# Weight sums moved from GpSimd to VectorE in single steps, four sets in the first pair, output weights loaded at two earlier places

## The chip, the cores and the metric

The kernel runs on one core of one Trainium2 chip. The metric is the device time of one execution in microseconds (us), lower is better. Five engines work side by side, each through its own list in order: TensorE (PE), VectorE (DVE), ScalarE (ACT), GpSimd (POOL) and SyncE (SP), which here issues nearly all transfers between the chip's memory and the on-chip buffers.

## The reference

Attention in chunks of 64 keys, then a feed-forward block with RMS norm and SiLU gate, in float32. N = 4608 tokens, model width 512, inner width 1536.

```python
scores = scale * np.matmul(q_c, k_c.transpose(0, 1, 2, 4, 3))   # chunks of 64
attn = softmax(scores)
x = np.matmul(attn, v_c)        # heads side by side: 4608 x 512
xn = x / sqrt(mean(x * x) + 1e-6) * rms_g
g, val = xn @ w_gate, xn @ w_val
out = (g * sigmoid(g) * val) @ w_out
```

## The kernel before

**Tiles and pairs.** Tokens go in nine tiles of 512. Tile 0 is done plainly while the weights are brought into a split form (a high part that the PE takes exactly and a rest, three matmuls for one product). The other eight form four pairs, b = 0 to 3. A pair multiplies as a 2x2 block matrix with seven products, P1 to P7, instead of eight; each needs its own sums of weight blocks and of inputs.

**The first pair, b = 0,** still takes its gate and value weights plainly: two blocks (tiles) of twelve inner columns f, `gate_into`, ps_g and ps_v in the profile (L587). Its output stage, `down_pair`, uses seven products with the output weights wo (L1066), which `out_load` (L972) brings from their split home osd, 1 MB each. **From b = 1 on** `up_pair` (L854) takes seven products over pieces i = 0 to 5, with weights wr that `ring_load` (L846) brings from the split home wsd three ahead, 1 MB for two products, then `down_pair`.

**The weight sets.** For P3, P5, P6 and P7 of each piece i, `sides(i)` loads the weight blocks (w<-wfd, L751, two transfers of 512 KB), forms four sums on POOL (L745), and `save_split` then does four times: a cast on ACT (L774), a store of the high part (wsd<-side, L775), a subtraction on DVE (L776), a store of the rest (wsd<-w, L777). The high part, `side`, lies in a pool of four buffers that it shares with `gh`, the high part of the output stage's inputs.

**Attention of the next tiles** runs in between, by units of 256 tokens: scores (PE ps_s, L266), maxima, subtraction and sums on DVE (L336, L337, L348), exponential on ACT (L343), a transpose on DVE (e, L360), which goes through memory (away_e<-e, L362, then eight transfers eT<-away_e, L371), then values (PE ps_o, L388). The result xu goes through the norm and through memory too (away_x, x<-away_x, L423, L430).

**Order.** A step counter runs one step per group of matmuls: 48 steps for a pair's first stage. Tables (SIDE_AT, LATE_SIDE_AT, UNIT_AT, PAIR_AT and others) say at which step a part of the side work is written down. PE's order is that of the code; a scheduler orders the other engines in the first stages, all are in written order in the output stages. Every DMA also waits for the one that stands eight places before it on SP, since eight completion counters go round, and whatever stands behind it on SP waits with it. Steps of SIDE_AT count from the first pair's start; its second block begins at step 24.

Of the kernel before, what the change touches and what calls it, by code (L numbers as in the profile page):

```python
# [43 lines left out]
X_AT = 5, 12, 13, 14, 15, 16, 25, 27, 30  # L44
OUT_AT = -2, 0, 3, 7, 11, 15
SAVE_AT = 5, 9, 13, 17, 21, 25
SIDE_AT = 29, 35, 41
LATE_SIDE_AT = 0, 6, 12
IN_ORDER = {
    mybir.EngineType.PE,  # L50
    mybir.EngineType.Activation,
# [29 lines left out]
def tile_chunk_attn_swiglu(  # L81
# [10 lines left out]
    nc = tc.nc  # L92
# [32 lines left out]
    def urgent():  # L125

        return tc.high_priority(offset=URGENT)
# [600 lines left out]
    def save_up(i):  # L728
        one, two = parts_of(2 * i), parts_of(2 * i + 1)
        save_side(i, P1, one[:, :, :, :KH])  # L730
        save_side(i, P2, one[:, :, :, KH:])
        save_side(i, P4, two[:, :, :, KH:])
# [7 lines left out]
    def sides(i):  # L740

        at = {}

        def total(out, one, two, op):
            nc.gpsimd.tensor_tensor(out, one, two, op=op)  # L745

        def load():
            both = big([P, 2, 2, DM], F32, "w")
            for f in range(2):
                w = both[:, f]  # L750
                nc.sync.dma_start(w.rearrange("p m c -> p (m c)"), wfd[2 * i + f])  # L751
                for half in range(2):
                    at[f + 1, half + 1] = w[:, :, half * KH : (half + 1) * KH]

        def sums():
            total(at[2, 2], at[2, 1], at[2, 2], ALU.add)
            total(at[2, 1], at[1, 1], at[2, 1], ALU.subtract)
            total(at[1, 1], at[2, 2], at[1, 1], ALU.subtract)
            total(at[1, 2], at[1, 2], at[1, 1], ALU.subtract)

        def split():
            save_split(i, P7, at[2, 1])
            save_split(i, P5, at[2, 2])
            save_split(i, P6, at[1, 1])
            save_split(i, P3, at[1, 2])

        return [load, sums, split]

    def save_split(i, p, w):

        n = 7 * i + p
        dst = wsd[n // 2][:, n % 2].rearrange("p (a m c) -> p a m c", a=2, m=2)
        part = tmp.tile([P, 2, KH], F32R, tag="tmp", name="side")
        nc.scalar.copy(part, w)  # L774
        nc.sync.dma_start(dst[:, 0], part.bitcast(F32))  # L775
        nc.vector.tensor_tensor(w.bitcast(F32R), w, part.bitcast(F32), op=ALU.subtract)  # L776
        nc.sync.dma_start(dst[:, 1], w)  # L777

    def big(shape, dtype, name):
        return wts.tile(shape, dtype, tag="wts", name=name)  # L780
# [188 lines left out]
    def out_load(n):  # L969
        t = big([P, PER, 2, OH], F32R, "wo")  # L970
        part = t[:, : osd[n].shape[1]].rearrange("p n a c -> p n (a c)")
        nc.sync.dma_start(part.bitcast(F32), osd[n])  # L972
        return t
# [212 lines left out]
    at = {}  # L1186

    def plan(n, todo):
        at.setdefault(n, []).append(todo)

    for n, u in enumerate(range(4, 10)):
        after_it = LAST_STEPS if u == 9 else PAIR_STEPS
# [3 lines left out]
    for i in range(NPR):  # L1196
# [9 lines left out]
            plan(OUT_AT[i] + (min(k, 2) if OUT_AT[i] >= 0 else 0), part)  # L1206
        plan(SAVE_AT[i], lambda i=i: save_up(i))
    for i, n in enumerate(SIDE_AT):
        for after_it, f in zip((0, 1, 3), sides(i)):
            plan(n + after_it, f)  # L1210

    def before(n):
# [42 lines left out]
    for b in range(NB):  # L1255
        t = 1 + 2 * b
        gts, wos, tt, sums, ready = [], [], [], [], []

        def first_splits():
            for g, _ in gts[:2]:  # L1260
                split_high(g[:, 0, 0], ready)
            split_low(gts[0][0][:, 0, 0], ready[0])

        if b == 0:

            one, two, late = x_sides(x, x2, st)
            for n, f in enumerate(one[:2]):
                plan(UNIT_AT[3] + PAIR_STEPS[-1] + 4 + n, f)
            for n, f in zip(X_AT, one[2:] + two[:1] + two[4:] + two[1:4]):
                plan(2 * UP + n, f)  # L1270
            early = {n: list(todo) for n, todo in enumerate(late)}
            for i, n in enumerate(LATE_SIDE_AT):
                for after_it, f in zip((0, 1, 3), sides(len(SIDE_AT) + i)):
                    early.setdefault(n + after_it, []).append(f)
            step = Steps(at)
            gs = []
            for f in range(NF):
                if f % 2 == 0:
                    gs.append(big([P, 2, 2, TT], F32, "g"))
                gate_into(f, gs[-1][:, f % 2, 0], step, f == NF - 1)  # L1280
            with urgent():
                for dt in range(NDT):
                    x_split(dt, blocks(x)[:, :, dt], slice(0, TT))
            for f in range(NF):
                i = f // 2
                if f % 2 == 0 and sums:
                    sums.pop()()
                end = f == NF - 1
                if end:
                    gts.append((gs[i], None))  # L1290
                    wos.append(out_load(0))
                    wos.append(out_load(1))
                gate_into(f, gs[i][:, f % 2, 1], step, f == 0, first_splits if end else None)
                if f % 2:
                    if end:
                        gts.pop()
                    gts.append((gs[i], sum_later(i, gs[i], tt, sums)))
        else:
            at = early
            early = {}  # L1300
            if b + 1 < NB:
                u = 2 * t + 4
                for n in range(4):
                    home = (lambda: x2) if n > 1 else (lambda: x)
                    for k, f in enumerate(unit_steps(u + n, home)):
                        after_it = LAST_STEPS if b == 1 and n == 3 else PAIR_STEPS
                        at.setdefault(max(PAIR_AT[n] + after_it[k], 0), []).append(f)
                one, two, late = x_sides(x, x2, st)
                for n, f in enumerate(one[:2]):
                    at.setdefault(PAIR_AT[1] + PAIR_STEPS[-1] + 4 + n, []).append(f)  # L1310
                for n, f in zip(X_AT, one[2:] + two[:1] + two[4:] + two[1:4]):
                    at.setdefault(7 * NPR + n, []).append(f)
                early = {n: list(todo) for n, todo in enumerate(late)}
            step = Steps(at)
            for i in range(NPR):
                last_part = first_splits if i == NPR - 1 else None
                gts.append(up_pair(i, step, wos, tt, sums, last_part))
        loaded[0] = 0
        ordered.__exit__(None, None, None)
        ordered = tc.manual_schedule(engines=IN_ORDER)  # L1320
        ordered.__enter__()
        down_pair(t, gts, wos, step, b + 1 < NB, sums, ready)
        ordered.__exit__(None, None, None)
        ordered = tc.manual_schedule(engines={mybir.EngineType.PE})
        ordered.__enter__()
# [53 lines left out]
```

## Time and profile before

| what | value |
|---|---|
| median of 3 runs | 932.96 us (932.84 to 936.49) |
| profiled execution | 933.43 us, span 931.6 us |
| PE busy | 881.9 us of the span |
| DVE busy | 648.1 us |
| ACT busy | 486.5 us |
| POOL busy | 196.1 us, of it 33.5 us in the 24 sums of L745 |
| second block of the first pair | ends at 290.3 us |
| first output stage | to 363 us, then the second pair's first stage |

All other numbers come from the one profiled execution; its own time lies 0.5 us above the median. A row of a timeline has the start in us from the span's start, the length, the engine, the line, the operation, output and inputs without buffer numbers, the size and the count of like instructions run together; in brackets the idle time of the engine ahead of it and what ended it. SPq is SP's own queue: the row is the time over which transfers were issued, not when they landed.

### The profile page before, as it was taken

The page shows a single profiled execution, that of the slowest core. Times are in us where ns is not written, and L with a number is a line of the kernel's source. Part 1 is how long each engine was busy: PE and PEld are TensorE (multiplying, and loading weights), DVE is VectorE, ACT ScalarE, POOL GpSimd, SP SyncE. Part 2 cuts the span into 40 slices and gives each one's busy share as a digit, 9 for nine tenths or more (in the row PEclk, how much of TensorE's full clock was granted, in tenths as well). Part 3 has the DMA queues.
Part 4 walks back from the last instruction along what each step waited for, and adds up shares of the span by engine and source line. Part 5 has one row for each costly group of instructions (what it writes and reads, how often), then busy time and mean ns, then how long its engine had stood idle before and what let it go on. Part 6 is the DMA issues. An engine that isn't in the chain of part 4 may idle for free.

```text
span 931.6 us, 17562 instructions
## 1 busy us (share of the span) xinstructions
PE 881.9 (95%) x6792; PEld 718.4 (77%) x6792; DVE 648.1 (70%) x1030; ACT 486.5 (52%) x807; POOL 196.1 (21%) x165
## 2 busy tenths in 40 slices
PE   4899999999996999895999999999999999999998
PEld 3688888788875787774888887887887878888886
DVE  6999897665863897764565997666668964334776
ACT  5998955445552754442474754444747532222452
POOL 0004020000520003534134001332340013432201
PEclk9799999999998999987999999999999999999999
DMA  9698999876778668897898678676875686335442
GB/s 353 267 349 336 321 334 304 265 242 205 241 251 284 263 242 320 276 312 233 307 332 317 228 279 327 253 215 246 295 241 225 243 336 251 142 138 202 203 159 90
DMA packets 87379, 242.85 MB, mean 261 GB/s; under 512 B 9088, under 2 KB 45440, under 8 KB 71808
## 3 DMA queue, kind: packets, MB, share of 16 engines
q1 hardware_dynamic: 86240, 241.21, 73.0%
q8 instruction: 53, 0.87, 0.4%
q10 hardware_dynamic: 1056, 0.52, 0.2%
q14 instruction: 30, 0.25, 0.1%
HBM read 178.26 MB, written 63.44 MB: 259 GB/s over the span
## 4 chain that ended last, share of the span: by engine, by line
PE 85%; DMA 7%; DVE 3%; ACT 2%; issue 1%; SPq 1%; POOL 0%; DVEq 0%; ACTq 0%; POOLq 0%
PE ps_c L854 11%; PE ps_a L854 10%; PE ps_b L854 10%; PE ps_v L587 8%; PE ps_g L587 8%; PE ps_c L1066 7%; PE ps_a L1066 7%; PE ps_b L1066 6%; PE ps_d L854 6%; PE acc L658 4%; DMA wr<-wsd 3%; PE ps_d L1066 3%; PE ps_o L388 2%; PE ps_s L266 2%; DMA osd<-side 2%
## 5 line engine op out<-in xcount | busy, mean ns | idle before, releaser
L854 PE MATMUL ps_c<-xp,wr 128*128 128x512 f32 x432 | 106.4, 396 | 0.2 <-DMA wr<-wsd 0.2
L854 PE MATMUL ps_a<-xp,wr 128*128 128x512 f32 x432 | 104.8, 390 | 0.6 <-DMA wr<-wsd 0.6
L854 PE MATMUL ps_b<-xp,wr 128*128 128x512 f32 x432 | 104.5, 391 | 0.0
L854 PEld LDWEIGHTS ps_c<-xp,wr 128*128 128x128 f32 x432 | 82.0, 191 | 17.9 <-issue 0.5
L854 PEld LDWEIGHTS ps_a<-xp,wr 128*128 128x128 f32 x432 | 80.9, 188 | 18.5 <-DMA wr<-wsd 1.7
L854 PEld LDWEIGHTS ps_b<-xp,wr 128*128 128x128 f32 x432 | 80.6, 188 | 17.2 <-DVE p L947 0.2
L587 PE MATMUL ps_g<-xh,parts 128*128 128x512 f32 x272 | 91.2, 396 | 0.6 <-ACT xh L512 0.6
L587 PE MATMUL ps_v<-xh,parts 128*128 128x512 f32 x272 | 90.4, 393 | 0.0
L977 ACT CAST gh<-g 128x512 fp32r<-128x512 f32 x96 | 58.2, 621 | 55.8 <-PE ps_b L1066 17.7
L982 DVE TENSOR_TENSOR gl<-g,gh 128x512 fp32r<-128x512 f32 x96 | 65.7, 694 | 26.1 <-PE ps_a L1066 14.4
L854 PE MATMUL ps_d<-xp,wr 128*128 128x512 f32 x216 | 54.9, 405 | 11.2 <-DMA wr<-wsd 11.2
L1066 PE MATMUL ps_a<-gh,wo 128*128 128x512 f32 x192 | 53.9, 396 | 8.1 <-DMA wo<-osd 8.1
L982 DVE TENSOR_TENSOR gl<-tt,gh 128x512 fp32r<-128x512 f32 x72 | 55.8, 787 | 8.0 <-PE ps_a L1066 4.1
L587 PEld LDWEIGHTS ps_g<-xh,parts 128*128 128x128 f32 x272 | 51.7, 190 | 12.0 <-ACT xh L512 1.0
L587 PEld LDWEIGHTS ps_v<-xh,parts 128*128 128x128 f32 x272 | 51.3, 189 | 11.0
L913 ACT ACTIVATE p<-p 128x512 f32<-128x512 f32 x36 | 22.7, 632 | 67.7 <-POOL p L935 50.1
L854 PEld LDWEIGHTS ps_d<-xp,wr 128*128 128x128 f32 x216 | 41.9, 195 | 20.6 <-issue 11.6
L977 ACT CAST gh<-tt 128x512 fp32r<-128x512 f32 x72 | 42.7, 621 | 26.0 <-PE ps_b L1066 12.5
L945 POOL TENSOR_TENSOR g<-u,u 128x512 f32<-128x512 f32 x18 | 23.2, 1287 | 155.2 <-DVE u L941 71.1
L935 POOL TENSOR_TENSOR p<-p,p 128x512 f32<-128x512 f32 x36 | 46.9, 1314 | 36.5 <-DVE p L934 29.5
L587 PE MATMUL ps_g<-xl,parts 128*128 128x512 f32 x136 | 53.6, 394 | 0.0
L587 PE MATMUL ps_v<-xl,parts 128*128 128x512 f32 x136 | 53.2, 391 | 0.0
(161 smaller groups left out, 1793.5 us busy)
## 6 DMA issues: line engine op xcount, KB each, us to landing
wr<-wsd SPq DMA_DIRECT2D x63, 1024.0 KB, 7.7
wo<-osd SPq DMA_DIRECT2D x40, 1024.0 KB, 8.3
raw<-w_up_dram SPq DMA_DIRECT2D x12, 1024.0 KB, 9.8
vt<-v_dram SPq DMA_DIRECT2D x18, 512.0 KB, 5.7
wsd<-parts SPq DMA_DIRECT2D x18, 512.0 KB, 6.0
qt<-qT_dram SPq DMA_DIRECT2D x17, 512.0 KB, 6.0
kt<-kT_dram SPq DMA_DIRECT2D x17, 512.0 KB, 6.4
away_e<-e SPq DMA_DIRECT2D x28, 256.0 KB, 2.3
```

What stands on the lines that cost most here:

```text
L266: nc.tensor.matmul(st["s"][j][c * CH : (c + 1) * CH, pr], st["q"][rows, pr, tok : tok + CH], st["k"][rows, pr, tok : tok + CH], start=True ...
L388: nc.tensor.matmul(st["o"][(2 * c + t) * Q : (2 * c + t + 1) * Q, h * D : (h + 1) * D], eT[c][rows, t, h], vt[rows, c, h], start=True, sto ...
L587: nc.tensor.matmul(ps, a[f][:, cols], b[dt], start=(dt == 0 and i == 0), stop=(dt == NDT - 1 and i == 2),)
L658: nc.tensor.matmul(acc[s], a[:, cols], b, start=(f == 0 and i == 0), stop=(f == NF - 1 and i == 2),)
L854: nc.tensor.matmul(ps, w[:, a, m, cols], xp[:, b, kt], start=start and kt == 0 and i == 0, stop=stop and kt == 1 and i == 2, skip_group_ch ...
L913: nc.scalar.activation(t, t if src is None else src, AF.Silu)
L935: nc.gpsimd.tensor_tensor(kp["p5"], kp["p1"], kp["p5"], op=add)
L945: nc.gpsimd.tensor_tensor(g[:, 0, 1], kp["u2"], kept[0]["u2"], op=mult)
L977: nc.scalar.copy(gh, src)
L982: nc.vector.tensor_tensor(gl, src, pair[0].bitcast(F32), op=ALU.subtract)
L1066: nc.tensor.matmul(banks[m][name], w[:, (0, 1, 0)[k], m * P : (m + 1) * P], (gh, gh, gl)[k], start=opens and i == 0 and k == 0, stop=not ( ...
```

## The change

The four sums of a set go to DVE. A set has five steps instead of three: load; two sums (step 2); split P7 and the third sum (3); split P5 and the fourth sum (4); splits P6 and P3 (5). Four sets start in the first pair, at steps 27, 31, 35 and 39 (before: three, at 29, 35, 41), and two in the second pair at 3 and 11 (before: three at 0, 6, 12). The first two wo are loaded at f = 8 and f = 10 of the second block, before both at f = 11. Lines of the new kernel lie one to five further down: L745 is L746, L751 L752, L775 L780, L776 L781, L777 L782, L846 L851, L972 L977, L371 L372, L362 L363, L360 L361, L935 L940, L939 L944, L945 L950, L951 L956.

```diff
-SIDE_AT = 29, 35, 41
-LATE_SIDE_AT = 0, 6, 12
+SIDE_AT = 27, 31, 35, 39
+LATE_SIDE_AT = 3, 11
+OUT_LOAD_AT = 8, 10
...
         def total(out, one, two, op):
-            nc.gpsimd.tensor_tensor(out, one, two, op=op)
+            nc.vector.tensor_tensor(out, one, two, op=op)
...
         def sums():
             total(at[2, 2], at[2, 1], at[2, 2], ALU.add)
             total(at[2, 1], at[1, 1], at[2, 1], ALU.subtract)
+
+        def first():
+            save_split(i, P7, at[2, 1])
             total(at[1, 1], at[2, 2], at[1, 1], ALU.subtract)
+
+        def second():
+            save_split(i, P5, at[2, 2])
             total(at[1, 2], at[1, 2], at[1, 1], ALU.subtract)
 
-        def split():
-            save_split(i, P7, at[2, 1])
-            save_split(i, P5, at[2, 2])
+        def third():
             save_split(i, P6, at[1, 1])
             save_split(i, P3, at[1, 2])
 
-        return [load, sums, split]
+        return [load, sums, first, second, third]
...
     for i, n in enumerate(SIDE_AT):
-        for after_it, f in zip((0, 1, 3), sides(i)):
+        for after_it, f in zip((0, 2, 3, 4, 5), sides(i)):
             plan(n + after_it, f)
...
                 if end:
                     gts.append((gs[i], None))
-                    wos.append(out_load(0))
-                    wos.append(out_load(1))
+                if f in OUT_LOAD_AT:
+                    wos.append(out_load(len(wos)))
```

The same change to the steps, (0, 1, 3) to (0, 2, 3, 4, 5), stands where LATE_SIDE_AT is used. PE's order is the same as before.

**SP at the end of the second block.** Numbers after wsd, osd and wfd tell pieces in memory apart, those after away_e units. Before, the eT of the unit stood ahead of the second set's stores and of all wo:

```order
L371 DMA eT<-away_e_3243 32x2x256 x4
L371 DMA eT<-away_e_3250 32x2x256 x4
L775 DMA wsd_149<-side 128x512
L777 DMA wsd_149<-w 128x2x256
L775 DMA wsd_147<-side 128x512
L777 DMA wsd_147<-w 128x2x256
L775 DMA wsd_148<-side 128x512
L777 DMA wsd_148<-w 128x2x256
L775 DMA wsd_149<-side 128x512
L777 DMA wsd_149<-w 128x2x256
L972 DMA wo<-osd_161 128x2048
L972 DMA wo<-osd_162 128x2048
```

Now, from the second away_e of the same unit on (the first wo stands seven rows ahead of it):

```order
L363 DMA away_e_3281<-e 128x512
L780 DMA wsd_153<-side 128x512
L782 DMA wsd_153<-w 128x2x256
L431 DMA x_1481<-away_x_3248 32x4x256 x4
L780 DMA wsd_151<-side 128x512
L782 DMA wsd_151<-w 128x2x256
L977 DMA wo<-osd_162 128x2048
L372 DMA eT<-away_e_3274 32x2x256 x4
L372 DMA eT<-away_e_3281 32x2x256 x4
L780 DMA wsd_151<-side 128x512
L782 DMA wsd_151<-w 128x2x256
L780 DMA wsd_152<-side 128x512
```

The second wo and two splits of set three moved ahead of the eT.

**DVE at the same place,** from the end of that unit's softmax to its second transpose. Before:

```order
L337 TENSOR_TENSOR e<-ps_s_3135,mx 128x4x2x32
L348 TENSOR_REDUCE rs<-e 128x8
L349 TENSOR_SCALAR rs<-rs 128x8
L360 STREAM_TRANSPOSE e<-e 128x512
L350 RECIPROCAL rs<-rs 128x8
L648 TENSOR_TENSOR g<-ps_v,sg 128x512
L903 TENSOR_TENSOR tt<-g 128x512
L348 TENSOR_REDUCE rs<-e 128x8
L776 TENSOR_TENSOR w<-w,side 128x2x256
L349 TENSOR_SCALAR rs<-rs 128x8
L360 STREAM_TRANSPOSE e<-e 128x512
```

Now, from the first sum of set three to the second transpose:

```order
L746 TENSOR_TENSOR w<-w 128x2x256
L350 TENSOR_SCALAR rs<-rs 128x8
L361 STREAM_TRANSPOSE e<-e 128x512
L746 TENSOR_TENSOR w<-w 128x2x256
L649 TENSOR_TENSOR g<-ps_v,sg 128x512
L351 RECIPROCAL rs<-rs 128x8
L349 TENSOR_REDUCE rs<-e 128x8
L781 TENSOR_TENSOR w<-w,side 128x2x256
L350 TENSOR_SCALAR rs<-rs 128x8
L361 STREAM_TRANSPOSE e<-e 128x512
```

Between the softmax's last subtraction and the first of these stand six instructions: a g of L649, three subtractions and a sum of set two, and a row sum (rs). Two sums of set three moved in front of the transposes.

**POOL in the second pair's first piece.** p, u and g are partial results of a product. Before:

```order
L935 TENSOR_TENSOR p_4047<-p_3989,p_4047 128x512
L745 TENSOR_TENSOR w<-w 128x2x256 x3
L935 TENSOR_TENSOR p_4049<-p_3991,p_4049 128x512
L939 TENSOR_TENSOR g<-p_4049,p_4047 128x512
L951 TENSOR_TENSOR g<-p_3991,p_3989 128x512
```

Now:

```order
L940 TENSOR_TENSOR p_4067<-p_4016,p_4067 128x512
L940 TENSOR_TENSOR p_4069<-p_4018,p_4069 128x512
L944 TENSOR_TENSOR g<-p_4069,p_4067 128x512
L956 TENSOR_TENSOR g<-p_4018,p_4016 128x512
L147 TENSOR_TENSOR ri<-ss,mhalf 128x1
```

The three sums between the two p are gone.

**SP in the second pair, at the last set's stores.** Before:

```order
L775 DMA wsd_158<-side 128x512
L777 DMA wsd_158<-w 128x2x256
L775 DMA wsd_159<-side 128x512
L777 DMA wsd_159<-w 128x2x256
L430 DMA x<-away_x_4523 32x4x256 x4
L362 DMA away_e_4597<-e 128x512
L362 DMA away_e_4604<-e 128x512
L846 DMA wr<-wsd_150 128x2048
L371 DMA eT<-away_e_4597 32x2x256 x4
```

Now:

```order
L780 DMA wsd_158<-side 128x512
L782 DMA wsd_158<-w 128x2x256
L431 DMA x<-away_x_4521 32x4x256 x2
L363 DMA away_e_4587<-e 128x512
L363 DMA away_e_4594<-e 128x512
L851 DMA wr<-wsd_150 128x2048
L780 DMA wsd_158<-side 128x512
L782 DMA wsd_158<-w 128x2x256
L780 DMA wsd_159<-side 128x512
```

Two of the set's four splits moved behind the wr (wsd 10, here 150), and with them stand ahead of the eT.

More of the change, by code (lines that the diff above doesn't have):

```diff
@@ L1272, in tile_chunk_attn_swiglu @@
             for i, n in enumerate(LATE_SIDE_AT):
-                for after_it, f in zip((0, 1, 3), sides(len(SIDE_AT) + i)):
+                for after_it, f in zip((0, 2, 3, 4, 5), sides(len(SIDE_AT) + i)):
                     early.setdefault(n + after_it, []).append(f)
```

## The prediction, made before the run

> **What bounds the kernel now.** I read the page's head, then the waits of PE, then PE's timeline around each wait, then SP, VectorE (DVE) and GpSimd (POOL) at the same places.
>
> ```profile
> span 931.6 us, 17562 instructions
> PE 881.9 (95%) x6792; PEld 718.4 (77%) x6792; DVE 648.1 (70%) x1030; ACT 486.5 (52%) x807; POOL 196.1 (21%) x165
> ```
>
> PE is busy for 881.9 of 931.6 us, and the change leaves PE's instructions alone. So it can win or lose only in PE's 49.7 us of idle time and in stretches that run at a low clock after an idle time.
>
> ```profile
> PE ps_d L854 <- DMA wr<-wsd: 11.2, 1, 11.2
> PE ps_a L1066 <- DMA wo<-osd: 8.1, 1, 8.1
> PE ps_o L388 <- DMA eT<-away_e: 4.9, 2, 4.1
> ```
>
> These three waits lie where the change works. PE's timeline gives their places (start, length, instruction, idle time before it and its end):
>
> ```profile
> 261.29 1.48 PE L388 MATMUL ps_o<-vt,eT 64*32 64x64 f32 x128
> 265.65 1.04 PE L266 MATMUL ps_s<-kt,qt 64*64 64x64 f32 x54
> 267.85 0.44 PE L266 MATMUL ps_s<-kt,qt 64*64 64x64 f32 x10 [1.16 <-issue]
> ...
> 298.42 2.05 PE L1066 MATMUL ps_a<-gh,wo 128*128 128x512 f32 x4 [8.15 <-DMA wo<-osd]
> 301.25 1.81 PE L388 MATMUL ps_o<-vt,eT 64*32 64x64 f32 x128
> ...
> 397.11 0.27 PE L388 MATMUL ps_o<-vt,eT 64*32 64x64 f32 x2 [4.07 <-DMA eT<-away_e]
> 398.23 2.43 PE L388 MATMUL ps_o<-vt,eT 64*32 64x64 f32 x126 [0.85 <-DMA eT<-away_e]
> 400.60 4.89 PE L854 MATMUL ps_c<-xp,wr 128*128 128x512 f32 x12
> 405.33 2.88 PE L854 MATMUL ps_b<-xp,wr 128*128 128x512 f32 x12
> 408.14 1.16 PE L266 MATMUL ps_s<-kt,qt 64*64 64x64 f32 x64
> ...
> 417.53 2.88 PE L854 MATMUL ps_b<-xp,wr 128*128 128x512 f32 x12
> ...
> 439.76 5.46 PE L854 MATMUL ps_d<-xp,wr 128*128 128x512 f32 x12 [11.19 <-DMA wr<-wsd]
> ```
>
> Twelve matmuls take 2.88 us normally, but 4.89 after the eT wait and 5.46 after the wr wait. So the eT place costs 4.9 + 2.0 = 6.9 us, the wr place 11.2 + 2.6 = 13.8. At the wo place, ps_o (301.25) could have started 1.4 us after 290.3 (298.42 - 8.15; the first product is six matmuls, half of 2.8), so 9.6 us hang there. More than 30 us isn't to be had.
>
> SP issues the transfers in program order:
>
> ```profile
> 254.31 3.69 SPq L371 DMA_DIRECT2D eT<-away_e  x8
> ...
> 282.38 3.88 SPq L371 DMA_DIRECT2D eT<-away_e  x8
> ...
> 291.43 2.91 SPq L972 DMA_DIRECT2D wo<-osd  x4
> ...
> 430.87 0.46 SPq L846 DMA_DIRECT2D wr<-wsd  x1
> 433.43 6.51 SPq L371 DMA_DIRECT2D eT<-away_e  x8
> ```
>
> wo was issued when PE already wanted it. wr (wsd 10) was issued at 430.87, 2.3 us after PE began to wait (439.76 - 11.19 = 428.57), behind the last set's eight stores. Median times from issue to landing, the last number:
>
> ```profile
> wr<-wsd SPq DMA_DIRECT2D x63, 1024.0 KB, 7.7
> wo<-osd SPq DMA_DIRECT2D x40, 1024.0 KB, 8.3
> ...
> eT<-away_e SPq DMA_DIRECT2D x112, 64.0 KB, 3.3
> ...
> w<-wfd SPq DMA_DIRECT2D x12, 512.0 KB, 6.0
> wsd<-side SPq DMA_DIRECT2D x24, 256.0 KB, 4.2
> ```
>
> **The change, part by part.**
>
> *The sums.* 24 leave POOL, 24 come to DVE. The nearest DVE row is the split's subtraction, of the same size, the second of these:
>
> ```profile
> L745 POOL TENSOR_TENSOR w<-w 128x512 f32<-128x512 f32 x24 | 33.5, 1394 | 42.3 <-DMA w<-wfd 31.0 <-PE ps_a L854 7.6 <-PE ps_c L854 2.3
> ...
> L776 DVE TENSOR_TENSOR w<-w,side 128x512 fp32r<-128x512 f32 x24 | 19.0, 815 | 5.3 <-ACT side L774 5.3
> ```
>
> At 0.7 to 0.8 us each DVE gains 17 to 20 us, beside PE's matmuls: by itself nothing. What counts is who stands behind a sum in DVE's order: POOL's 31.0 us of waiting for w<-wfd now happen in DVE's queue, with softmax and the emptying of PSUM behind them.
>
> *The second block and wo.* DVE's rows of before:
>
> ```profile
> 268.67 0.71 DVE L336 TENSOR_REDUCE mx<-ps_s 128x4 f32<-128x256 f32 x2
> ...
> 270.64 0.74 DVE L337 TENSOR_TENSOR e<-ps_s,mx 128x256 f32<-128x256 f32 x2
> ...
> 280.69 0.70 DVE L360 STREAM_TRANSPOSE e<-e 128x512 f32<-128x512 f32 x1
> ```
>
> First, the eT of 254.31 come later: one sum and one subtraction ahead of the second transpose (1.4 us) and two stores ahead on SP (1.3 us) put their issue at 257.0 to 260.7, and the last lands after 261.29: a new wait of some 1.6 us (bounds 0 and 4). ps_s moves to 267.3. Then the four maxima and subtractions, in before done at 271.4, have three sums and a subtraction among them (2.8 us), the first waiting for w: done at 276.5. Six more instructions: 280.6. Then a sum of set three waits for its w, whose second half stands on SP behind a store of set two (an estimate: about 275.8, after the second split; plus 6.0 to land): 281.8. Ten instructions more, 4.5 us, to the second transpose: 286.3 instead of 281.4. After it SP stores away_e and the first part of set three (0.6), and the second wo can't be issued until that store has landed, as each transfer waits for the one eight places before it: 286.9 + 4.2 = 291.1. The eight eT now stand behind this wo, and the last waits for its landing: 291.1 + 8.3 = 299.4, plus 3.3 = 302.7. The first wo, issued near 278, lands at 286 and is in time: the 8.15 us go, but PE runs 1.4 us and meets ps_o, which waits for eT until 302 instead of 301.25. So the wo term is +0.7, bounds -8 (eT in time) and +5 (a later load of w by the 5 us by which DVE is late).
>
> *The eT of the second pair.* Of before, POOL and DVE:
>
> ```profile
> 382.31 4.36 POOL L745 TENSOR_TENSOR w<-w 128x512 f32<-128x512 f32 x3
> 386.62 1.29 POOL L935 TENSOR_TENSOR p<-p,p 128x512 f32<-128x512 f32 x1
> ...
> 387.94 0.69 DVE L947 TENSOR_TENSOR p<-p,ps_d 128x512 f32<-128x512 f32 x1 [3.79 <-POOL p L935]
> ...
> 390.48 0.70 DVE L360 STREAM_TRANSPOSE e<-e 128x512 f32<-128x512 f32 x1
> ```
>
> The transposes stood behind a DVE instruction that waited 3.79 us for POOL, where three sums ran first. In the new order nothing stands between POOL's two p, and the third set is already done. The second transpose comes near 384, 6.5 us earlier; away_e lands by 387, and the eT, now mixed with two stores, are issued until about 390.5 and land about 393.5, where PE wants them at 393.04. Gain 6.4 of 6.9 (bounds 0 and 6.9).
>
> *wr of wsd 10.* I count from ps_s (408.14 of before). PE wants wr at +20.4; it was issued at +22.7. Now it stands behind the second transpose, away_e and two of the four splits. The transpose follows an L927 that needs ps_b (417.53 + 2.8, +12.2); L927, a small one and the transpose take 1.6, two away_e 0.9: issue near +14.6. With 7.7 to the landing, or the 8.9 that it took (439.76 - 430.87), that is +22.3 to +23.5: a wait of 2.5 instead of 11.2. Five of the eight eT behind it wait for its landing; the last is issued 1.9 later (0.46 each) and lands 3.3 later, and PE gets there after 2.8 of ps_d: 2.4 us of new waiting. Gain 13.8 - 2.5 - 2.4 = 8.9 (bounds 4 and 13.8).
>
> *Clock.* The new waits are short. The row after 1.16 us of idle time lies in the first stretch here, at full clock; the last holds the one after the eT wait (columns: window, busy times of PE, PEld, DVE, ACT and POOL, granted clock, DMA share, GB/s):
>
> ```profile
> 265.00:270.00 5.00, 3.84 (x76) 2.94 (x75) 3.79 (x8) 2.78 (x5) 1.07 (x2) 1.00 1.09 320
> ...
> 275.00:280.00 5.00, 5.00 (x24) 4.14 (x23) 3.77 (x4) 2.25 (x3) 4.76 (x4) 1.00 0.33 104
> ...
> 400.00:410.00 10.00, 10.00 (x138) 7.92 (x121) 7.48 (x10) 4.83 (x12) 4.09 (x4) 0.77 0.90 292
> ```
>
> For waits of 1.6, 2.5 and 2.4 us that is between 0 and 2.0 each; nearest to the short one, I take 1.0 in all. The Trainium skill ("TensorE: Matmul & The Clock Gate", the section on the HAM clock gate) says the clock falls to half after an idle window of about 3.4 us; the halved rows after 4.9 and 11.2 us agree, and by it these waits would cost nothing and the sum would be 1.0 less.
>
> *Sum*, against the profiled execution's 933.43 us: +0.7 - 6.4 - 8.9 + 1.0 = -13.6, so 919.8. That execution lies 0.5 above the median of the runs, 932.96; from the median it is **919.4 us**.
>
> **The rivals.**
> - *All three waits go.* The eT of the second block would have to land 8 us sooner, which only a wo issued near 285 allows, and wr 3 us sooner. -8 - 6.9 - 13.8 gives 904. For it: DMA is only 0.33 busy at 275 to 280, above; against it: the store and wo ahead of eT.
> - *Only one of the second pair's gains comes*: 933 - 6.4 or - 8.9, 924 to 927.
> - *The waits only move.* With each step put 5 us later by a w that lands late (set four's before the eT, set five's before the transposes) the eT keep their 4.9 and wr comes at +20 instead of +14.6: gain 0 to 4, 929 to 936. For it: the 31.0 us that POOL waited for w.
> - *Slower.* The same hold of DVE at w in the second block, one mechanism: every us that the third set's w lands after 281.8 moves the second transpose, the store, wo and eT one for one. Landing 9 us late instead of 6.0 after issue, with each of the two sets before it late by as much, puts eT at 311, +9; with nothing won later that is 942. It decides from eT at 306 where the second pair brings nothing, but only from 320 where it brings what I forecast. Against it: the loads there are 512 KB each, beside 1 MB transfers that land in 8.3.
>
> **Chances.** Under 0.5% (4.7 us) no change can be told in this kernel. My forecast (912 to 924) 0.48; all gone (below 912) 0.14; one gain only (924 to 928.3) 0.13; waits moved 0.15; slower (above 937.6) 0.10. So faster 0.75, same 0.15, slower 0.10. The likeliest one's own range is 912 to 924; the range of 8 in 10 reaches down to 906 and up to 934, into the moved waits.
>
> **What would show it.** Right: no wait for wo at PE's first product of the first pair's output stage, but a wait of some 9 us at ps_o for eT right behind it; no L745's successor on POOL; at the second pair's first ps_o hardly a wait; wr at ps_d down from 11.2 to 1 to 4 and some at the ps_o behind it; a small new wait at ps_o near 261. Wrong: eT of the second block landing before 295 (then faster than said) or after 306, DVE waiting for w<-wfd by more than 5 us at a time, or wr of wsd 10 issued later than 17 us after its ps_s.

## The result, and the profile after

The changed kernel takes **924.61 us** (median of 4 runs, 922.36 to 925.78), the kernel before on the same chip 934.67 us (4 runs, 932.84 to 936.49): a ratio of 0.9889, 95% interval 0.9856 to 0.9923, so 1.1% faster. The forecast was 919.4, range 906 to 934, so the time lies inside it; it is 0.6 us above the 912 to 924 that the prediction gave to its likeliest course. One run of an experiment below, 996.64 us at a granted clock of 0.842 where all others had 0.973 or more, is a slow one, and no ratio counts it. The profiled execution took 923.88 us, 9.55 less than the one before.

The head of the page after, and its waits of PE (us in total, times, longest):

```profile
span 922.1 us, 17546 instructions
...
PE 878.1 (95%) x6792; PEld 716.1 (78%) x6792; DVE 652.8 (71%) x1054; ACT 486.4 (53%) x807; POOL 162.8 (18%) x141
```

```profile
PE ps_o L389 <- DMA eT<-away_e: 9.3, 4, 7.8
PE ps_d L859 <- DMA wr<-wsd: 6.3, 1, 6.3
```

The sums have left POOL (196.1 to 162.8 us). On DVE the 24 take 16.2 us, yet its total grew by only 4.7 (648.1 to 652.8), since its other rows together became shorter. PE has the same matmuls. The line for wo is gone and the longest eT wait has grown from 4.1 to 7.8; wr at ps_d still waits 6.3. PE's timeline after, at the places that the prediction names:

```profile
261.05 1.49 PE L389 MATMUL ps_o<-vt,eT 64*32 64x64 f32 x128
...
290.32 1.09 PE L1071 MATMUL ps_a<-gh,wo 128*128 128x512 f32 x4
...
299.72 0.39 PE L389 MATMUL ps_o<-vt,eT 64*32 64x64 f32 x2 [7.85 <-DMA eT<-away_e]
300.79 2.38 PE L389 MATMUL ps_o<-vt,eT 64*32 64x64 f32 x126 [0.69 <-DMA eT<-away_e]
...
393.36 1.48 PE L389 MATMUL ps_o<-vt,eT 64*32 64x64 f32 x128
...
400.44 1.16 PE L267 MATMUL ps_s<-kt,qt 64*64 64x64 f32 x64
...
427.14 4.80 PE L859 MATMUL ps_d<-xp,wr 128*128 128x512 f32 x12 [6.27 <-DMA wr<-wsd]
431.87 1.48 PE L389 MATMUL ps_o<-vt,eT 64*32 64x64 f32 x128
...
437.71 1.27 PE L267 MATMUL ps_s<-kt,qt 64*64 64x64 f32 x64 [1.37 <-issue]
440.44 3.02 PE L859 MATMUL ps_c<-xp,wr 128*128 128x512 f32 x12 [1.46 <-DMA wr<-wsd]
```

A row without a bracket started with no idle time. The first output product (290.32) starts at once, and ps_o behind it now waits; the second pair's first ps_o (393.36) waits for nothing. SP at the same places (start, time of issue):

```profile
276.56 0.46 SPq L977 DMA_DIRECT2D wo<-osd  x1
...
290.08 0.50 SPq L977 DMA_DIRECT2D wo<-osd  x1
290.67 8.72 SPq L372 DMA_DIRECT2D eT<-away_e  x8
...
417.79 0.44 SPq L851 DMA_DIRECT2D wr<-wsd  x1
```

The eight eT take 8.72 us to issue behind a wo, where they took 3.88 before. SP's own waits from 276 to 302 us say what for:

```profile
SPq L372 <- DMA wo<-osd: 3.4, 1, 3.4
...
SPq L372 <- DMA wsd<-side: 1.5, 1, 1.5
```

Eight places round, the last of them waits for that wo to land, and one before it for a store of a set.

I take as marks the starts of ps_s and ps_o on PE, before and after:

| stretch of PE's timeline | before | after | difference |
|---|---|---|---|
| first pair, ps_s near 265.5 to the second pair's first ps_s (s) | 265.65 to 369.82 | 265.46 to 370.28 | +0.7 |
| s to the next ps_s, over the eT place | 38.32 | 30.16 | -8.2 |
| from there two units on, over the wr place | 408.14 to 479.85 | 400.44 to 469.52 | -2.6 |
| to the next ps_o | 26.1 | 25.8 | -0.3 |
| the rest, same order in both | 425.65 | 426.78 | +1.1 |

### The profile page after: what moved, and what is told of

Its sections match the earlier page's. It is cut to its first block, busy times and chain, and to the rows that moved or that the text cites. A ratio compares the mean times of both kernels' runs of the same rounds, so it can differ in the third digit from the quotient of the medians.

```text
span 922.1 us, 17546 instructions
## 1 busy us (share of the span) xinstructions
PE 878.1 (95%) x6792; PEld 716.1 (78%) x6792; DVE 652.8 (71%) x1054; ACT 486.4 (53%) x807; POOL 162.8 (18%) x141
## 4 chain that ended last, share of the span: by engine, by line
PE 78%; DMA 9%; DVE 6%; ACT 3%; issue 2%; SPq 1%; POOL 0%; DVEq 0%; ACTq 0%; POOLq 0%
PE ps_b L859 9%; PE ps_a L859 9%; PE ps_c L859 9%; PE ps_g L588 7%; PE ps_v L588 7%; PE ps_c L1071 7%; PE ps_b L1071 6%; PE ps_a L1071 6%; PE ps_d L859 4%; PE acc L659 4%; PE ps_d L1071 3%; DMA wr<-wsd 3%; PE ps_o L389 2%; PE ps_s L267 2%; DMA wsd<-w 1%
## 5 line engine op out<-in xcount | busy, mean ns | idle before, releaser
L588 PEld LDWEIGHTS ps_g<-xh,parts 128*128 128x128 f32 x272 | 51.6, 190 | 12.3 <-ACT xh L513 1.0
L950 POOL TENSOR_TENSOR g<-u,u 128x512 f32<-128x512 f32 x18 | 23.2, 1289 | 182.5 <-ACT u L918 90.8
L147 POOL TENSOR_TENSOR ri<-ss,mhalf 128x1 f32<-128x1 f32 x28 | 15.6, 564 | 219.4 <-ACT ss L146 207.8
```

The costliest lines, as they stand in the source:

```text
L147: nc.gpsimd.tensor_tensor(ri, ss, half, op=ALU.pow)
L588: nc.tensor.matmul(ps, a[f][:, cols], b[dt], start=(dt == 0 and i == 0), stop=(dt == NDT - 1 and i == 2),)
L950: nc.gpsimd.tensor_tensor(g[:, 0, 1], kp["u2"], kept[0]["u2"], op=mult)
```

## The experiments

Three questions: why did the gain at wo vanish, what removed the eT wait, and what still holds wr. Each kernel was timed beside the kernel before; ratios are to it, with 95% intervals. The medians of the kernel before lie between 934.67 and 935.51 us in the five series, its single runs between 932.83 and 939.54. Differences of a few us between two kernels can't be told from their medians alone, so the timelines decide as much. A timeline is one execution, though: up to 400 us two of the experiments below (last set on POOL, last set at step 17) have the order of the changed kernel, and the first stretch of the table took 104.8 us in its execution, 109.1 and 108.4 in theirs. The changed kernel is called "the change" here.

**wo at its old place within the change.**

```diff
-                if f in OUT_LOAD_AT:
-                    wos.append(out_load(len(wos)))
+                if f == NF - 1:
+                    wos.append(out_load(0))
+                    wos.append(out_load(1))
```

> The changed kernel, but both first output weights loaded at f = 11 as before. Theory (the second wo ahead of the eT is what made PE wait 7.85 us at ps_o): the eT are issued near 289.5 and land by 297, no wait for them any more, but the first wo is issued near 295, lands near 303, and PE waits some 12 us for it at 290.3; ps_o starts near 305 instead of 300.8: 3 to 5 us slower than the changed kernel, about 928 to 929. Rival (the eT are late through DVE's softmax alone, whatever stands with them on SP): the eT land near 300 as now, and wo lands near 303 to 305 behind: again a little slower, but with a wait for eT of its own. Rival 2 (the output weights don't matter): same time within 1 us.

Measured 927.83 us, 0.9919 (0.99 to 0.9938), 3.2 over the change, though the two intervals overlap. Its PE:

```profile
299.91 2.04 PE L1071 MATMUL ps_a<-gh,wo 128*128 128x512 f32 x4 [10.27 <-DMA wo<-osd]
...
302.74 1.81 PE L389 MATMUL ps_o<-vt,eT 64*32 64x64 f32 x128
```

The wait stands at wo again, eT is in time, and ps_o starts at 302.7 instead of 299.7. So within the change the earlier wo mostly trades one wait for the other. The first stretch of the table takes 106.9 us here: without the earlier wo, the rest of the change costs it 2.7 us.

**Second wo behind the eT.**

```diff
-OUT_LOAD_AT = 8, 10
+OUT_LOAD_AT = 8, 11
```

> The changed kernel, but the second output weight is loaded at f = 11 instead of 10, so behind the eT and the rest of set three; the first stays at 8. Theory (eT wait for the second wo, by order and by the completion counter eight places before): eT issued at 290 to 294, landed by 297; wait at ps_o down from 8.5 to 4 to 5 us; the second wo then lands near 303, where PE wants it at about 302: 0 to 2 us. Net 2 to 4 us faster than the changed kernel. Rival (eT late through the second transpose and the x<-away_x that wait ahead of them): ps_o still starts after 299.5, no gain within 1 us.

Measured 923.07 us, 0.9874 (0.985 to 0.9898). Its PE and SP:

```profile
295.32 0.39 PE L389 MATMUL ps_o<-vt,eT 64*32 64x64 f32 x2 [2.61 <-DMA eT<-away_e]
```

```profile
291.25 4.01 SPq L372 DMA_DIRECT2D eT<-away_e  x8
```

Issued at the same time, 291, the eT take 4.0 instead of 8.7 us without a wo ahead, and ps_o starts 4.4 us earlier: the second wo is what PE waited for through eT. It isn't the luck of one execution: in the four timelines with this order up to 370 us (this one and three further down) ps_o starts at 295.3 to 297.7, in the three with the order of the change at 299.7 to 304.1. Part of this is lost again: from ps_o to the second pair's ps_s it takes 72.1 us, in the change 70.6.

**Only the wo places, on the kernel before.** Sums, sets and their places as before.

```diff
-                if end:
-                    ...
-                    wos.append(out_load(0))
-                    wos.append(out_load(1))
+                if f in (8, 10):
+                    wos.append(out_load(len(wos)))
```

> The kernel before with one change: the first two output weights loaded at f = 8 and 10. Theory (a load put ahead of the eT on SP makes the eT late): the wait of 8.2 us for wo goes, but the second wo stands right ahead of the eT, which then land when it has landed. In this order DVE has fewer sums, away_e is stored by 282 and the wo issued at about 283, so eT land near 291 to 293 and ps_o waits 0 to 2 us instead of starting at 301: 6 to 9 us gained at that place, total 925 to 929. Rival (eT land as late as in the changed kernel, near 300): total 933 to 936.

Measured 925.03 us, 0.9888 (0.9868 to 0.9908): as much as the whole change. PE, then SP:

```profile
290.44 1.19 PE L1066 MATMUL ps_a<-gh,wo 128*128 128x512 f32 x4 [1.29 <-ACT gh L977]
...
292.03 1.48 PE L388 MATMUL ps_o<-vt,eT 64*32 64x64 f32 x128
...
387.31 0.39 PE L388 MATMUL ps_o<-vt,eT 64*32 64x64 f32 x2 [3.79 <-DMA eT<-away_e]
...
430.74 4.80 PE L854 MATMUL ps_d<-xp,wr 128*128 128x512 f32 x12 [12.02 <-DMA wr<-wsd]
```

```profile
277.75 0.37 SPq L972 DMA_DIRECT2D wo<-osd  x1
278.82 8.18 SPq L371 DMA_DIRECT2D eT<-away_e  x8
```

Here too the eT stand behind the second wo, and their issue takes 8.18 us. But they are issued 12 us earlier than in the change, 278.82 against 290.67, and are in time. The second pair's first ps_s comes at 360.1, 9.7 us earlier than before; the first stretch of the table takes 95.3 us, 8.9 less. The two later waits stay. So the earlier wo is worth some 9 us by itself, and beside the rest of the change it is gone.

**Only the engine, on the kernel before.**

```diff
-            nc.gpsimd.tensor_tensor(out, one, two, op=op)
+            nc.vector.tensor_tensor(out, one, two, op=op)
```

> The kernel before with one change: the sums on DVE, at the old places and steps, and the output weights as before. Theory (the eT wait of 4.9 us came from POOL's sums between two p's): that wait and its low clock go, up to 8 us; the wr of wsd 10 still stands behind all eight stores, so its wait of 11.2 stays within 3 us, and the wo wait of 8.2 stays: 925 to 931. Rival (the places matter, not the engine): sums of two sets crowd DVE at the same spot, the second transpose comes as late as before, 932 to 938.

Measured 927.54 us, 0.9921 (0.9897 to 0.9945). The second pair's first ps_o (389.3) loses its 4.07 us eT wait (0.36 is left), and the wr wait stays, at 12.10. The wo wait, expected to stay at 8.2, is 4.68; why isn't shown.

**All but the engine: the change with its sums on POOL.** The same line turned round.

```diff
-            nc.vector.tensor_tensor(out, one, two, op=op)
+            nc.gpsimd.tensor_tensor(out, one, two, op=op)
```

> The changed kernel with all sums back on POOL; places, single steps and output weights as changed. Theory (engine and places both needed): at the second pair's first values POOL again has sums of set four between its p's, so 2 to 5 us of wait for eT come back; wr of wsd 10 behind two splits whose sums take 1.3 us each: wait 6 to 9; total 927 to 932. Rival (the places alone made the gain, since set three is gone from the second pair): no eT wait there, 922 to 926.

Measured 927.12 us, 0.9919 (0.9897 to 0.994). PE:

```profile
302.70 0.39 PE L389 MATMUL ps_o<-vt,eT 64*32 64x64 f32 x2 [7.59 <-DMA eT<-away_e]
...
396.46 1.48 PE L389 MATMUL ps_o<-vt,eT 64*32 64x64 f32 x128
...
430.69 5.46 PE L859 MATMUL ps_d<-xp,wr 128*128 128x512 f32 x12 [6.70 <-DMA wr<-wsd]
```

No eT wait at 396.46 either: each half, engine or places, removes it alone. The wr wait is 6.70, near the change's 6.27, so its gain is one of the places. And the 7.59 us at 302.70 stand there with no sum on DVE: what takes the wo gain back is where the sets and their steps stand, whichever engine forms the sums. The unit's second transpose on DVE shows how: it starts at 275.06 with the wo places alone, at 282.23 in the change and at 283.47 here. In the change sums and subtractions of the sets stand ahead of it on DVE. Here the subtractions alone do, and one of them waits 3.09 us for its cast. The second wo follows the transpose by 2.0 us with the wo places alone (277.75) and by 7.1 in the change (290.08), where the stores of a set stand ahead of it on SP. So of the 12.3 us by which this wo is later, 7.2 come about on DVE and 5.1 on SP.

**The last set's sums on POOL, the rest as in the change.**

```diff
-            nc.vector.tensor_tensor(out, one, two, op=op)
+            (nc.gpsimd if i == 5 else nc.vector).tensor_tensor(out, one, two, op=op)
```

> The changed kernel, but the last set's four sums (second pair, piece 5) go back to POOL; the other five sets stay on DVE. Theory (four sums in DVE's list between the softmax and its second transpose put wr of wsd 10 at +17.3 us after ps_s instead of the forecast +14.6): without their 2.6 us the transpose comes at +12.8 to +13.5, wr is issued at +14.6 to +15, PE's wait for it falls from 6.3 to 3.5 to 4, total 2 to 3 us faster. Rival (wr waits for the set's first two splits, which stand ahead of it on SP, and POOL's sums take 1.3 us each): the casts come later by 2 to 3 us, wr is issued no sooner, wait 6 to 9, same or up to 3 us slower.

Measured 927.13 us, 0.9912 (0.9896 to 0.9928). Its SP; its ps_s stands at 405.3, so wr at 422.99 is +17.7:

```profile
416.31 1.34 SPq L780 DMA_DIRECT2D wsd<-side  x2
418.74 1.57 SPq L782 DMA_DIRECT2D wsd<-w  x2
...
421.99 0.91 SPq L363 DMA_DIRECT2D away_e<-e  x2
422.99 0.42 SPq L851 DMA_DIRECT2D wr<-wsd  x1
```

The wait at ps_d is 6.38, as in the change (6.27). Without the sums the second transpose (416.84, 0.70 long) ends at +12.2 instead of the change's +16.1, and yet wr is no earlier: two splits' stores and two x<-away_x stand ahead of away_e and wr on SP. So taking the sums off VectorE gains nothing here, because the stores of the later splits take over the wait. It doesn't show that the sums on VectorE cost nothing; the next two runs bear on that. This run also shows the scatter: its program up to 400 us is that of the change, yet ps_o starts at 304.1 instead of 299.7.

**The last set later: loaded at step 17 instead of 11.**

```diff
-LATE_SIDE_AT = 3, 11
+LATE_SIDE_AT = 3, 17
```

> The changed kernel, but the last set starts at step 17 of the second pair instead of 11, so that its sums, splits and stores lie behind the softmax, the away_e and the wr of wsd 10. Theory (the last set is what delays this wr): wr issued at about +12 after ps_s, landed by +20 to +21, PE's wait for it 0 to 1 us, no low clock behind it, no follow-up waits of 1.4 and 1.5: 8 to 11 us faster than the changed kernel, 914 to 917. Rival (the transfers themselves, 9.3 us from issue to landing, are the limit): wait still 2 to 4, gain 3 to 5. Rival 2 (the set costs the next unit what it cost this one): a new wait for eT or wr some 28 us later takes back half or more.

Measured 927.58 us, 0.9912 (0.9892 to 0.9931). SP and PE, the last with ps_s at 403.12:

```profile
415.11 0.42 SPq L851 DMA_DIRECT2D wr<-wsd  x1
```

```profile
434.70 0.33 PE L267 MATMUL ps_s<-kt,qt 64*64 64x64 f32 x4 [3.55 <-DVE xu L403]
...
456.48 3.00 PE L859 MATMUL ps_a<-xp,wr 128*128 128x512 f32 x12 [2.01 <-DMA wr<-wsd]
...
464.04 0.27 PE L389 MATMUL ps_o<-vt,eT 64*32 64x64 f32 x2 [1.84 <-DMA eT<-away_e]
```

wr goes out at +12.0, 0.5 us behind the end of the second transpose (413.95, 0.70 long), and ps_d waits no more, but the set now meets xu, the next wr and the next eT. The waits moved, and the time with them.

**The last set loaded at its old step, summed and stored from step 19; second wo at f = 11.**

```diff
-OUT_LOAD_AT = 8, 10
+OUT_LOAD_AT = 8, 11
...
-                for after_it, f in zip((0, 2, 3, 4, 5), sides(len(SIDE_AT) + i)):
+                for after_it, f in zip(((0, 2, 3, 4, 5), (0, 8, 9, 10, 11))[i], sides(len(SIDE_AT) + i)):
```

> The changed kernel with the second output weight at f = 11, and the last set loaded at step 11 as now but with its sums and splits from step 19 on. In DVE's list all four sums still stand ahead of the second transpose, but no split and no store of the set stands ahead of the wr of wsd 10 on SP. It parts the two: if the four sums (2.7 us) are what delays wr, it is issued at +14.5 to +15 after ps_s and PE waits 3 to 4 us; if the splits and stores are, it is issued at +12 to +13 and PE waits 0 to 1.5. The splits then stand ahead of the next unit's work and may cost 1 to 4 us there.

One run: 921.97 us. DVE, SP, then PE:

```profile
413.76 0.70 DVE L361 STREAM_TRANSPOSE e<-e 128x512 f32<-128x512 f32 x1
```

```profile
414.92 0.42 SPq L851 DMA_DIRECT2D wr<-wsd  x1
```

```profile
420.78 2.88 PE L859 MATMUL ps_d<-xp,wr 128*128 128x512 f32 x12
```

wr goes out at +14.4 after ps_s (400.51) and has landed by 420.78, in 5.9 us at most; in the change it went out at +17.35 and took 9.35. That is neither branch of the expectation: the issue is that of the sums, the missing wait that of the splits. Again wr follows the transpose by 0.5 us, so in this order VectorE sets its issue. From the run before, with nothing of the set there, to this one with its load and sums, wr moves from +12.0 to +14.4; with splits and stores too, in the change, to +17.35. So the load and the sums cost this wr 2.4 us, the splits and stores 2.9 and, as it seems from these two executions, the slower landing. Later ps_a waits 3.58 us for a wr (450.98).

**The last set at step 22, then at 25; second wo at f = 11 in both.**

```diff
-LATE_SIDE_AT = 3, 11
-OUT_LOAD_AT = 8, 10
+LATE_SIDE_AT = 3, 22
+OUT_LOAD_AT = 8, 11
```

> The changed kernel with the second output weight at f = 11 (as in the run that moved only that) and the last set at step 22 of the second pair instead of 11: its sums now stand on DVE behind the next unit's softmax and both its transposes, not ahead of an xu as in the run with step 17. Theory (the last set costs PE whatever DVE work it stands in front of: at 11 the second transpose and wr, at 17 xu and so ps_s; in front of nothing urgent it is free): wr of wsd 10 issued at +12 after ps_s, no wait for it, the stretch from the second pair's second ps_s to its third values (now 68 to 69 us over two units) falls to 58 to 62, total 913 to 917. Rival (the set's 3 MB of transfers cost the same wherever they are): a new wait for eT or wr of 4 us or more behind it, total 920 to 924.

Measured 922.52 us (three runs), 0.9867 (0.9839 to 0.9896). No wr wait at ps_d, but 5.73 us for eT at 455.80, the first stores of the set being ahead of them. With 25 in place of 22:

> The changed kernel with the second output weight at f = 11 and the last set at step 25 of the second pair. On SP its loads stand behind the third unit's away_e and its eight stores behind that unit's eT; on DVE its sums stand behind that unit's transposes. At 22 the first stores stood ahead of the eT and cost 5.7 us there. Theory (the set costs what stands directly behind it in a queue, not a fixed amount of transfer time): no wait for wr at ps_d, none for eT at the third unit's values above 1 us; from the second ps_s of the second pair to the fourth 58 to 62 us (68 with step 11, 67 with 22); total 913 to 917. Rival (3 MB of transfers take their 8 to 9 us of PE time wherever they go, since the second pair's transfers fill most of the time): a wait of 4 us or more for wr or eT further on, total 920 to 924.

Measured **920.3 us**, 0.9829 (0.9807 to 0.9852). PE:

```profile
453.88 0.27 PE L389 MATMUL ps_o<-vt,eT 64*32 64x64 f32 x2 [0.98 <-DMA eT<-away_e]
```

From its ps_s (401.94) two units on it takes 62.0 us, against 69.1 in the change: the term that the prediction gave to wr is there to be had when the stores stand behind both wr and eT.

**The parts that gained, joined.** Before, with wo at 8 and 10, the first pair's three sets on POOL, the second pair's three on DVE, the last at step 25.

```diff
-LATE_SIDE_AT = 0, 6, 12
+LATE_SIDE_AT = 0, 6, 25
...
-            nc.gpsimd.tensor_tensor(out, one, two, op=op)
+            (nc.vector if i >= 3 else nc.gpsimd).tensor_tensor(out, one, two, op=op)
...
-                for after_it, f in zip((0, 1, 3), sides(len(SIDE_AT) + i)):
+                for after_it, f in zip(((0, 1, 3), (0, 1, 3), (0, 2, 4))[i], sides(len(SIDE_AT) + i)):
...
-                    wos.append(out_load(0))
-                    wos.append(out_load(1))
+                if f in (8, 10):
+                    wos.append(out_load(len(wos)))
```

> The parts that gained by themselves, without the fourth set: before, with wo at f = 8 and 10, the first pair's three sets and their sums left on GpSimd at 29, 35, 41, the three sets of the second pair summed on VectorE, the last of them at step 25 instead of 12. If the 9.5 us at wo stay won because nothing else is put into the second block, if the eT wait of the second pair (3.8 us and its low clock) goes with the engine of the sums, and if the wr wait (11.2) goes with the late last set, the three add up: 908 to 914 us, a ratio near 0.975, with ps_s of the second pair at about 360, no wait at its first ps_o and none at ps_d. Rival: the first 400 us share one queue and the transfers, so that what is won at one wait comes back at the next (VectorE held by w in the second pair, eT behind stores): 918 to 924, as the whole change.

Measured 922.75 us, 0.9861 (0.9838 to 0.9885): the rival's time. PE:

```profile
406.18 4.58 PE L854 MATMUL ps_b<-xp,wr 128*128 128x512 f32 x12 [2.27 <-DMA wr<-wsd]
...
430.31 4.60 PE L854 MATMUL ps_c<-xp,wr 128*128 128x512 f32 x12 [1.96 <-DMA wr<-wsd]
...
474.83 4.58 PE L854 MATMUL ps_d<-xp,wr 128*128 128x512 f32 x12 [3.74 <-DVE rs L349]
```

The wo gain holds (ps_s at 360.95, 9.3 us ahead of the change) and the eT wait of the second pair shrinks to 0.86 and 0.42. Then new waits of 2 to 4 us, each with a row at a low clock behind it, give it back: by 596.9 the lead is gone (the change: 596.5).

**The same, with the second set from step 12 and summed eight steps later.**

```diff
-LATE_SIDE_AT = 0, 6, 25
+LATE_SIDE_AT = 0, 12, 25
...
-zip(((0, 1, 3), (0, 1, 3), (0, 2, 4))[i]
+zip(((0, 1, 3), (0, 8, 10), (0, 2, 4))[i]
```

> As the kernel joined from the parts that gained, but the second pair's second set loaded at step 12 and summed eight steps later, so that VectorE never meets a w that has not landed. If VectorE's waits for w are what costs in the second pair, 1 to 4 us faster than the joined kernel, 906 to 912; if the transfers' places on SyncE decide, the same within 2 us or slower, since the second set's stores now come at step 20 to 22, just ahead of the last set's load.

Measured **919.56 us**, 0.9833 (0.9811 to 0.9855). Its PE:

```profile
441.44 4.58 PE L854 MATMUL ps_a<-xp,wr 128*128 128x512 f32 x12 [2.15 <-DMA wr<-wsd]
...
451.15 0.27 PE L388 MATMUL ps_o<-vt,eT 64*32 64x64 f32 x2 [2.41 <-DMA eT<-away_e]
...
458.95 0.85 PE L388 MATMUL ps_o<-vt,eT 64*32 64x64 f32 x35 [4.58 <-issue]
```

From 392.1 (ps_s) to 415.1 (ps_o) no wait is left, 6.4 us better than joined without the shift. But the VectorE reading isn't shown: in that stretch the joined kernel's PE waited for wr, in its timeline above. And the rows above take most of the lead over the change away: it is 18.2 us at one ps_s (419.5 against 437.7) and 3.0 at the next (466.5 against 469.5). What ended the 4.58 us I can't tell; the profile names no releaser.

The two best, 919.56 and 920.3, lie 0.5% under the change's median; their intervals (to 0.9855 and 0.9852) end where that of the change begins (0.9856), so this is likely but at the edge of what these runs can tell.

## Why the prediction was right, and where it was off

- *Second block and wo: forecast +0.7, measured +0.7 by the marks; the mechanism held, the figure is luck.* The wait for wo went and ps_o waited for eT, to 299.72 and 300.79 where 302 was said, because the second wo went out at 290.08 (said: 291.1) ahead of the eT. That this wo is the cause is shown by the run with it at f = 11 (ps_o 4.4 us earlier). But the chain up to it was another. I had VectorE wait for set three's w until 281.8 and finish the second transpose at 286.3; that w was there by 278.43, and the transpose ended at 282.94, 3.4 us early. I then had the wo go out 4.8 us behind that, after a store had landed; it took 7.1, and among the rows ahead of it an x waited 1.9 us for away_x to land, which I hadn't counted. The two errors offset. And in the two other executions with this order the stretch came out at +4.9 and +4.2, not +0.7. The rival *all three waits go* needed a wo near 285; with the wo places alone it came at 277.75, and that wait did go.
- *A new wait of 1.6 at 261: wrong, none.* ps_o at 261.05 has no bracket: the eT went out at 255.30 to 259.39, not at 257.0 to 260.7.
- *eT of the second pair: forecast 6.4, measured 8.2.* No wait is left. I counted the low clock behind the wait only at ps_c; ps_o itself had run 2.43 us instead of the 1.48 it takes now, and that is 1.0 of the 1.8 missed. The reason was half told: POOL's three sums were in the way, but both DVE's sums with the old places and POOL's sums with the new places clear it.
- *wr of wsd 10: forecast 8.9, measured 2.6. This is the step that failed in size.* I put the issue at +14.6 after ps_s and the landing 7.7 to 8.9 later; it went out at +17.35 and took 9.35. So the wait is 6.27 where I had 2.5: 2.75 us more from the issue, 1.0 from the landing. DVE shows the issue:

```profile
413.99 0.68 DVE L927 TENSOR_TENSOR u<-ps_b,p 128x512 f32<-128x512 f32 x1
414.59 0.68 DVE L781 TENSOR_TENSOR w<-w,side 128x512 fp32r<-128x512 f32 x1
415.19 0.68 DVE L927 TENSOR_TENSOR u<-ps_b,p 128x512 f32<-128x512 f32 x1
...
415.86 0.71 DVE L361 STREAM_TRANSPOSE e<-e 128x512 f32<-128x512 f32 x1
```

I let the first L927 start when ps_b is done, at +12.2, with one L927 ahead of the transpose, which so ended at +13.8. But VectorE had no idle time from 401.8 (+1.3) on, with the set's sums and two of its subtractions in its list: the first L927 started at +13.55, a subtraction and a second L927 stood ahead of the transpose, and it ended at +16.1. The runs agree: +12.0 without the set, +14.4 with its load and sums, +17.35 with its splits too. With the sums on POOL wr was no earlier (+17.7), since the stores ahead of away_e then set it; with the splits moved away it landed in 5.9 us. So the term was bound by the set's sums, splits and stores, which I costed at nothing ahead of wr and not at all beside its landing. The 2.4 us of new eT wait behind ps_d, which I did charge, didn't come (431.87, no bracket); instead 1.37 and 1.46 came before ps_s and ps_c. In sum 13.8 - 6.3 - 1.9 (the low clock of 427.14) - 1.4 - 1.5 = 2.7, against 2.6 by the marks.
- *Clock: forecast 1.0.* The waits of 6.27 and 7.85 brought low rows (4.80 for 2.88, 2.38 for 1.48), those of 1.37 and 1.46 none. They are within the terms above.
- *Sum:* -13.6 said, -9.55 measured; -10.6 of it up to the mark at 495 us, and +1.1 in the rest, where the order is the same, which is within the scatter of single executions.
- *Rivals.* *One gain only* (924 to 927) is what happened in time: the eT gain whole, the wr gain a fifth. *Waits only move* describes the second block and, in the runs with a later last set, the second pair. *Slower*, by DVE held at w: DVE did meet a late w in the second block, but for 1.23 us at set two and no more:

```profile
270.10 0.69 DVE L746 TENSOR_TENSOR w<-w 128x512 f32<-128x512 f32 x1 [1.23 <-DMA w<-wfd]
```

What I didn't see in the profile of before: that the wo places by themselves were worth some 9 us. I costed wo, sums and sets only as one step. In the first stretch of the table, 104.2 us before, the wo places alone give 95.3 (95.8 and 95.6 in the two joined kernels), all the rest without them 106.9, both together 104.8 to 109.1. So apart they are -9 and +3, the latter from one execution, together +1 to +5. The prices don't add: beside the sets the second wo goes out 12 us later, and the eT behind it.

## What to carry to other kernels

When several edits meet in one stretch of a shared in-order queue, their prices don't add: here -9 and +3 became +1 to +5. Cost the new order as a whole, and each edit alone beside it, since the better part may be had without the rest. A small transfer that PE waits for should not stand behind a 1 MB load or a set's stores unless it is issued early enough, since it waits for their landing too: eT issued at 278.82 behind a wo were in time, those at 290.67 were not. In the joined kernel, where the transfers are 0.80 to 1.02 busy from 400 to 480 us, the waits that were removed came back further on; look for the place where the moved bytes can go at all.

## What the runs showed of the hardware that I had not expected

A short wait can cost more than itself. After waits of 1.96, 2.15 and 2.27 us the next twelve matmuls took 4.58 to 4.60 us instead of 2.88, after one of 2.01 us only 3.00. The traces show why. In each the granted clock is 1.00 or 0.50, and it changes only at the ends of steps of 3.41 us that follow one another through the whole execution. Two such steps of the joined kernel, in and behind its 2.27 us wait (columns as in the prediction's windows: length, busy times of PE, PEld, DVE, ACT and POOL, granted clock, DMA share, GB/s):

```profile
403.52:406.94 3.42, 1.15 (x5) 0.67 (x4) 2.81 (x7) 3.39 (x6) 1.55 (x1) 1.00 0.98 400
406.94:410.35 3.41, 3.41 (x9) 2.67 (x8) 2.20 (x5) 0.86 (x2) 0.00 (x0) 0.50 0.61 178
```

And two of the run with the last set at step 17, over its 2.01 us wait (454.47 to 456.48):

```profile
452.13:455.54 3.41, 2.34 (x11) 1.60 (x9) 1.63 (x3) 1.26 (x2) 3.27 (x3) 1.00 0.88 288
455.54:458.96 3.42, 2.48 (x11) 2.08 (x12) 1.29 (x2) 0.59 (x1) 1.33 (x2) 1.00 1.16 320
```

The first wait lies in one step, PE is idle for 0.66 of it, and the next step runs at half clock. The second is parted by the end of a step, PE is idle for 0.31 and 0.27 of the two, and the clock stays. In the fourteen profiled executions, from 100 to 900 us, all 33 full-clock steps with PE idle for 0.56 or more were followed by a step at half clock; of those with 0.53 or less one was, at 0.48. So here it is the idle share of a step that counts, and a gap of 2 us is enough if one step holds it. The Trainium skill ("TensorE: Matmul & The Clock Gate", the section on the HAM clock gate) puts the fall after an idle window of about 3.4 us, which it says runs freely; the steps agree with the length and the free run, but here a window didn't have to be idle throughout. A forecast does well to charge a wait of 2 us with up to 1.7 more.

The landing of a 1 MB load differed with its neighbours: 9.35 us with four stores behind it on SP, at most 5.9 with only the small eT behind it, in one execution each.
